# A low part made by the matmul engine, two convolutions moved back to the vector engine, and a new order: local and global attention with a gated layer on one core

## The chip, the cores and the metric

The kernel runs on one core of a Trainium2 chip. Its engines each work through an instruction stream of their own: TensorE (PE, with the weight load PEld ahead of each matmul), VectorE (DVE), ScalarE (ACT), GpSimd (POOL) and SyncE (SP, which here issues loads). The metric is the time of one execution in microseconds; before the change it is 375.08 us (median of 3 runs, 374.77 to 375.1).

## What is computed

```python
# attention: 8 batches, 8 heads, 512 local and 32 global positions, head size 64
s_g = scale * q_g @ concat(k_g, k_l).T            # global queries see everything
out_g = softmax(s_g) @ concat(v_g, v_l)
s_ll = where(|i - j| <= 32, scale * q_l @ k_l.T, -1e9)
a_l = softmax(concat(scale * q_l @ k_g.T, s_ll))  # local: global keys and a window
out_l = a_l @ concat(v_g, v_l)
x = concat(out_g, out_l) as [batch, 544, 512]     # heads side by side
# gated layer
gate = sigmoid(sum_k conv_w[k] * x shifted by 4 - k positions)   # 5 taps, causal, per channel
out = (gate * (x @ w_val)) @ w_out
```

(The shapes in the kernel: 512 local positions and 32 global ones of each batch.)

## The kernel before

The work is cut into 32 **units**: one batch and two of the eight heads, so four units make a batch. A unit u goes through these steps, which are named as in the order table (line numbers are those of the profile):

- `s` (L474): 32 small fp32 matmuls give the scores of 16 blocks of 32 queries against 128 keys, into two banks of PSUM. An fp32 matmul shows as two records in the trace, so 64 records a unit.
- `mx` (L486, DVE) adds the mask and finds the maximum, `exp` (L493, ACT) exponentiates, `t` (L499, PE) transposes with the identity into PSUM, `tc` copies that to SBUF (L306 if on ACT, L308 if on DVE), `av` (L510, PE) multiplies with the values.
- `eps` and `norm` (L521 and L523, DVE) divide by the sum, giving `xs`; `xt` (L529, PE) transposes it, channels to partitions, into a bank; `xc` copies the bank to SBUF behind four columns of `halo`.
- `xh` rounds that x to the matmul's fp32r format (the high part), and `xl` (L561, DVE) subtracts: the low part is x minus its high part. The gated layer multiplies high and low parts separately, three products for one.
- The convolution: for units 4 to 31 a `tap` and four `conv` steps (L565, DVE). For the first `NPC = 4` units it is done on PE instead: `dg` (L577, ACT) scales the identity by a tap five times, `pc` (L588) are five fp32 matmuls of 128x512 with these diagonals (two records each), and `pco` copies the sum to SBUF as the gate.
- `sig` (L596, ACT) makes the gate's tanh.

A batch's gated layer follows: `g1` (L612) are 4 x 4 groups of three matmuls of 128x512, `gv` (L620, DVE) multiplies with the gate, `gh` and `gl` (L626, DVE) split into high and low parts, and `g2` (L634) are again 4 x 4 groups of three, `ob` scales and `st` stores. The global queries of a batch have their own steps (`gs`, `gmax`, `gexp`, `gt`, `gtc`, `gav`, `gnorm`, `gx`). The weights arrive in 64-bit floats and are turned into two fp32r parts by steps `w0.s0` to `w7.s7`, on DVE and ACT, in the first 80 us.

What sets the order is a table written out by hand, `ORDER`: a list of step names, each with its engine where there is a choice (`:ACT`, `:DVE`) and the PSUM bank that it takes (`@n`). The program emits the steps in that order, and each engine runs its own steps in the order in which they stand there, waiting for what a step needs. A step also waits for room: there are eight PSUM banks, ten tiles each for xh, xl and gate, three for pm and mx, and loads take their turn by the table too (`iq`, `iv`, `wi`).

The low part, as it is before:

```python
(G if plan.tasks[f"xl{u}"].eng == "POOL" else V).tensor_tensor(out=xs_l[u],
    in0=st[u]["xc"][:, KW - 1:], in1=xs_h[u].bitcast(F32), op=ALU.subtract)
```

Of the kernel before, what the change touches and what calls it, by code (L numbers as in the profile page):

```python
# [51 lines left out]
tc0.0:ACT z1.0@3 t1.1@3 tc0.1:ACT tc1.1:ACT t1.0@4 w0.s4 av0@1 s2@57 wi4 w0.s5 w0.s6 eps0:ACT norm0 tc1.0:ACT xt0@4
xc0:ACT w0.s7 gs0@02 mx2.0 exp2.0 dg1 halo0 w1.s0:DVE w0.high:DVE mx2.1 iq4 pc0.0@6 pc0.1 pc0.2 gmax0.0 w1.s1 av1@4
s3@70 gmax0.1 w1.s2 gexp0.0 w1.s3 w1.s4 iq5 exp2.1 t2.1@1 eps1:DVE norm1 t2.0@2 xt1@3 tc2.1:ACT gt0.0@4 mx3.0 mx3.1
exp3.1 w1.high:ACT exp3.0 xc1:DVE xh1:ACT tc2.0:DVE pc0.3 pc0.4 halo1 pco0:ACT w1.s5 w1.s6 av2@2 t3.0@1 eps2:DVE norm2
pc1.0@7 pc1.1 xt2@2 w1.s7 w4.s0:DVE w4.s1 tc3.0:ACT w4.s2 w4.s3 gtc0.0 w4.s4 w3.s0:ACT w3.s1 gexp0.1 iq6 iq7 w4.s5 dg2
pc1.2 t3.1@3 tc3.1:ACT w4.high:ACT s4@10 mx4.0 mx4.1 av3@4 xc2:ACT w4.s6 w4.s7 xh0:ACT gav0.0@6 gt0.1@1 eps3:ACT norm3
pc1.3 gtc0.1 wi5 gav0.1 w3.s2 s5@34 exp4.1 t4.1@0 geps0:ACT w3.s3 gnorm0 exp4.0 gx0@1 gxc0:ACT mx5.0 mx5.1 halo2:DVE
tc4.1:ACT w3.s4 w3.s5 iv4 xt3@6 xc3:ACT xh3:ACT w5.s0:ACT w5.s1 xl3 t4.0@2 tc4.0:ACT pc1.4 pc2.0@5 pc2.1 pc2.2
w3.high:ACT exp5.0 xl0 pco1:ACT exp5.1 gs1@03 dg3 iv5 iv7 iv6 w5.s2 w5.s3 w5.high:DVE gmax1.0 gexp1.0 av4@6 gmax1.1  # L60
eps4:ACT t5.0@2 tc5.0:ACT pc2.3 pc2.4 s6@04 w5.s4 fix1 w5.s5 w5.s6 pco2:ACT sig2 t5.1@1 w5.s7 halo3:ACT pc3.0@3
gexp1.1 tc5.1:ACT norm4 xt4@6 xc4:ACT mx6.0 exp6.0 mx6.1 exp6.1 w3.s6 xl1 w3.s7 av5@1 eps5:ACT s7@05 mx7.0 gt1.0@6
gtc1.0 w2.s0:DVE fix0 sig0 norm5 w2.s1 xh2:DVE pc3.1 iq8 pc3.2 g1.0.0.0@4 wi6 t6.0@6 exp7.0 w2.s2 w2.s3 w2.s4 xt5@0
xc5:ACT mx7.1 t6.1@7 tc6.1:ACT pc3.3 pc3.4 w2.s5 tc6.0:ACT pco3:ACT w2.high:ACT w6.s0:ACT av6@1 gav1.0@0 w2.s6 w2.s7
eps6:ACT norm6 iq9 s8@76 exp7.1 xl2 t7.0@5 mx8.0 mx8.1 exp8.1 t7.1@3 wi7 gt1.1@1 w7.s0:ACT tc7.1:DVE exp8.0 w6.s1
w6.s2 gtc1.1 g1.0.0.1 g1.0.0.2 g1.0.0.3 gv.0.0 gh.0.0:ACT w6.s3 w6.high:ACT w6.s4 w7.s1 g1.0.1.0@7 g1.0.1.1 xt6@6 sig3
g1.0.1.2 g1.0.1.3 iq10 iq11 w7.s2 g1.0.2.0@4 g1.0.2.1 w7.s3 w7.high:ACT w7.s4 w7.s5 sig1 w7.s6 w7.s7 xc6:ACT g1.0.2.2
g1.0.2.3 gl.0.0 w6.s5 g1.0.3.0@2 g1.0.3.1 g1.0.3.2 gv.0.1 gv.0.2 tc7.0:ACT av7@5 w6.s6 w6.s7 eps7:ACT norm7 xh4:ACT
gav1.1 gh.0.1:DVE s9@31 iv8 geps1:ACT gnorm1 gs2@46 gx1@0 tap6:ACT iv9 mx9.0 exp9.0 gmax2.0 gl.0.1 g1.0.3.3 g2.0.0.0@3
gh.0.2:ACT t8.0@4 gv.0.3 gh.0.3:DVE t9.0@5 gxc1:ACT xt7@0 tap5:DVE tc8.0:ACT tc9.0:ACT t8.1@2 g2.0.0.1 halo5:ACT  # L70
gl.0.2 g2.0.0.2 gl.0.3 g2.0.0.3 g2.0.1.0@4 g2.0.1.1 mx9.1 g2.0.1.2 iv11 exp9.1 tc8.1:ACT gexp2.0 conv5.0 xc7:DVE
tap7:ACT halo6:DVE t9.1@5 ob.0.0:ACT iq12 st.0.0 iv10 tc9.1:ACT g2.0.1.3 g2.0.2.0@2 ob.0.1:ACT conv6.0 conv6.1
halo7:DVE conv7.0 g2.0.2.1 gt2.0@0 gtc2.0 iq13 gmax2.1 st.0.1 conv5.1 g2.0.2.2 av8@3 eps8:ACT xh5:ACT conv6.2 conv6.3
conv5.2 conv5.3 av9@0 eps9:ACT norm8 s10@56 xl5 mx10.0 xt8@3 g2.0.2.3 g2.0.3.0@7 g2.0.3.1 g2.0.3.2 xh7:ACT g2.0.3.3
xh6:ACT exp10.0 norm9 t10.0@4 mx10.1 exp10.1 halo4:ACT conv7.1 iq14 t10.1@5 s11@01 xl6 ob.0.3:ACT iq15 gav2.0@7
tc10.1:ACT tc10.0:ACT tap4:DVE conv4.0 conv4.1 xt9@6 xl4 gexp2.1 gt2.1@4 sig5 mx11.0 g1.1.0.0@0 conv4.2 sig6 gtc2.1
gav2.1 geps2:ACT av10@4 xl7 conv4.3 sig4 eps10:ACT xc8:ACT xh8:ACT gnorm2 gx2@7 g1.1.0.1 g1.1.0.2 g1.1.0.3 xc9:ACT
xh9:ACT tap9:ACT ob.0.2:DVE g1.1.1.0@6 st.0.2 gxc2:DVE halo9:ACT norm10 st.0.3 mx11.1 exp11.1 tap8:DVE conv7.2 conv7.3
g1.1.1.1 g1.1.1.2 g1.1.1.3 g1.1.2.0@2 gv.1.0 gv.1.1 gh.1.0:DVE gl.1.0 t11.1@7 gh.1.1:ACT g1.1.2.1 gl.1.1 gs3@30
gmax3.0 s12@56 mx12.0 mx12.1 exp11.0 tc11.1:ACT t11.0@7 gexp3.0 g1.1.2.2 g1.1.2.3 g1.1.3.0@3 g1.1.3.1 xt10@4  # L80
# [833 lines left out]
```

## Time and profile before

| | |
|---|---|
| median of 3 runs | 375.08 us |
| profiled execution | 375.27 us |
| its span, first to last instruction | 373.5 us |
| PE busy | 359.2 us (96% of the span), 6349 matmul records |
| DVE busy | 317.9 us (85%) |
| ACT busy | 227.9 us (61%) |
| POOL busy | 0.8 us |
| DMA | 66.7 MB, mean 179 GB/s |

The span is the stretch from the first to the last instruction; what lies around it is 1.8 us. "Busy" counts an engine as busy while any of its instructions runs; matmuls are pipelined and their ends are modelled, so a matmul's own duration is longer than the step from one to the next, and the step is what a sum must use. In the chain of waits, "issue" is time in which an engine waited for nothing that the profile shows.

### The profile page before, as it was taken

What the parts mean: (1) busy time and instruction counts of PE and PEld (TensorE: products, weight loads), DVE (VectorE), ACT (ScalarE), POOL (GpSimd) and SP (SyncE); (2) the same over time, 40 slices, a digit from 0 to 9 for tenths busy, and PEclk for the clock granted to TensorE, in tenths of its full rate; (3) what the DMA queues carried; (4) which work ended last, traced back from release to release, by engine and by line L of the source; (5) the groups of instructions that cost most, each with busy time, mean ns of one, the idle gap of its engine ahead of it and who ended that gap; (6) DMA issues with size and microseconds to landing.
All of it is one profiled execution on the core that took longest, in us unless ns stands there. A gap on an engine that the chain in (4) does not pass through costs nothing.

```text
span 373.5 us, 14728 instructions
## 1 busy us (share of the span) xinstructions
PE 359.2 (96%) x6349; PEld 282.3 (76%) x6349; DVE 317.9 (85%) x1045; ACT 227.9 (61%) x586; POOL 0.8 (0%) x7
## 2 busy tenths in 40 slices
PE   7899989989899998999999999999999999999995
PEld 4566556868687886887877888888878888888894
DVE  4899888799988996999998897897889898797972
ACT  4789886476587375876568754685375567354040
POOL 0000000000000000000000000000000000000000
PEclk9999999999999999999999999999999999999999
DMA  7996584546841565942762854472920501011113
GB/s 280 400 396 221 167 323 134 162 153 220 352 146 52 193 217 224 333 186 107 259 237 68 320 218 162 184 270 90 336 85 32 215 4 58 2 56 73 42 65 105
DMA packets 17249, 66.74 MB, mean 179 GB/s; under 512 B 1952, under 2 KB 4000, under 8 KB 17184
## 3 DMA queue, kind: packets, MB, share of 16 engines
q1 hardware_dynamic: 12240, 57.12, 42.3%
q10 hardware_dynamic: 4944, 8.67, 6.4%
q8 instruction: 50, 0.82, 0.9%
q14 instruction: 15, 0.12, 0.1%
HBM read 56.87 MB, written 8.91 MB: 176 GB/s over the span
## 4 chain that ended last, share of the span: by engine, by line
PE 90%; DMA 4%; issue 2%; ACT 2%; SPq 1%; DVE 0%; DVEq 0%; ACTq 0%
PE psum L634 25%; PE psum L612 23%; PE psum L510 9%; PE psum L474 8%; PE psum L499 8%; PE psum L588 5%; PE psum L529 4%; DMA v<-in_vw_dram 3%; PE psum L439 3%; PE psum L400 2%; DMA wraw<-in_w_out_dram 2%; PE psum L419 2%; PE psum L421 1%; SPq L324 1%; PE psum L455 0%
## 5 line engine op out<-in xcount | busy, mean ns | idle before, releaser
L493 ACT ACTIVATE pm<-pm,mx 128x128 f32<-128x128 f32 x256 | 80.5, 392 | 14.6 <-DVE mx L486 14.2
L565 DVE SCALAR_TENSOR_TENSOR gate<-xc,cw,gate 128x512 f32<-128x512 f32 x112 | 82.8, 748 | 2.0
L486 DVE CUSTOM_DVE_ANT_0 pm<-psum,mask 128x128 f32<-128x128 f32 x256 | 57.3, 285 | 5.2 <-PE psum L474 5.1
L612 PE MATMUL psum<-xh,wvh 128*128 128x512 f32 x128 | 53.7, 419 | 0.0
L634 PE MATMUL psum<-woh,gh 128*128 128x512 f32 x128 | 52.6, 411 | 0.0
L634 PE MATMUL psum<-woh,gl 128*128 128x512 f32 x128 | 50.2, 392 | 1.5 <-issue 1.5
L634 PE MATMUL psum<-wol,gh 128*128 128x512 f32 x128 | 50.2, 392 | 1.4 <-issue 1.4
L612 PE MATMUL psum<-xl,wvh 128*128 128x512 f32 x128 | 50.6, 396 | 0.0
L612 PE MATMUL psum<-xh,wvl 128*128 128x512 f32 x128 | 50.1, 391 | 0.0
L499 PE MATMUL psum<-ident,pm 128*128 128x128 f32 x256 | 40.8, 280 | 0.3 <-issue 0.3
L474 PE MATMUL psum<-qk 64*32 64x128 f32 x2048 | 38.1, 278 | 1.9 <-issue 1.5
L306 ACT COPY pts<-psum 128x512 f32<-128x512 f32 x50 | 28.4, 582 | 18.3 <-PE psum L499 17.9
L510 PEld LDWEIGHTS psum<-v,pts 128*32 128x32 f32 x2048 | 30.5, 109 | 11.3 <-issue 4.6
L499 PEld LDWEIGHTS psum<-ident,pm 128*128 128x128 f32 x256 | 29.8, 140 | 9.9 <-issue 3.1
L510 PE MATMUL psum<-v,pts 128*32 128x65 f32 x2048 | 35.2, 221 | 1.9 <-ACT pts L306 1.2
L474 PEld LDWEIGHTS psum<-qk 64*32 64x32 f32 x2048 | 29.5, 107 | 9.6 <-issue 4.3
L299 ACT ACTIVATE ob<-psum 128x512 f32<-128x512 f32 x25 | 14.8, 595 | 28.3 <-PE psum L634 26.7
L634 PEld LDWEIGHTS psum<-wol,gh 128*128 128x128 f32 x128 | 24.2, 189 | 5.8 <-issue 1.8
L634 PEld LDWEIGHTS psum<-woh,gh 128*128 128x128 f32 x128 | 24.2, 189 | 5.8 <-issue 1.7
L612 PEld LDWEIGHTS psum<-xh,wvl 128*128 128x128 f32 x128 | 24.0, 188 | 5.5
L612 PEld LDWEIGHTS psum<-xh,wvh 128*128 128x128 f32 x128 | 24.2, 189 | 5.1 <-ACT pgt L427 0.4
L634 PEld LDWEIGHTS psum<-woh,gl 128*128 128x128 f32 x128 | 24.0, 188 | 5.2
(114 smaller groups left out, 541.9 us busy)
## 6 DMA issues: line engine op xcount, KB each, us to landing
v<-in_vw_dram SPq DMA_DIRECT2D x32, 975.0 KB, 6.2
qk<-in_qk_dram SPq DMA_DIRECT2D x32, 624.0 KB, 5.4
out_dram<-ob ACTq DMA_DIRECT2D x32, 256.0 KB, 2.3
wraw<-in_w_val_dram SPq DMA_DIRECT2D x4, 512.0 KB, 12.2
...
```

The lines of the kernel that those rows point to most:

```text
L299: A.activation(out=out, in_=in_, func=AF.Copy, scale=by)
L306: A.copy(out, in_)
L474: on_pe(T.matmul((sx, sy)[h][32 * j:32 * j + 32, i, :], qkt[rows, 32 * m:32 * m + 32], qkt[rows, k0:k0 + P], start=True, stop=True))
L486: V.tensor_tensor_reduce(out=pm[:, h, i, :], in0=s[:, i, :], in1=mask[:, i, :], op0=ALU.add, op1=ALU.min, scale=-SCALE, scalar=3.0e38, acc ...
L493: A.activation(out=pm[:, h, i, :], in_=pm[:, h, i, :], func=AF.Exp, bias=mx[:, c:c + 1], scale=-1.0)
L499: on_pe(T.transpose(pt[:, i, :], pm[:, h, i, :], ident))
L510: on_pe(T.matmul(ax[32 * j:32 * j + 32, h, E1 * i:E1 * i + E1], pts[:, h, i, 32 * j:32 * j + 32], vt[:, block_win(4 * i + j), h, :], start ...
L529: on_pe(T.transpose(xt[:, P * i:P * i + P], xs[:, i].rearrange("p h d -> p (h d)"), ident))
L565: V.scalar_tensor_tensor(out=acc, in0=xc[:, k:k + SL], scalar=cw[:, u % NDT, k:k + 1], in1=acc, op0=ALU.mult, op1=ALU.add)
L588: on_pe(T.matmul(st[u]["pc"], diag[(u * KW + k) // NDT][:, (u * KW + k) % NDT, :], st[u]["xc"][:, k:k + SL], start=(k == 0), stop=(k == KW ...
L612: on_pe(T.matmul(box["pv", e], w[:, e, t * P:t * P + P], x, start=(t == 0 and q == 0), stop=(t == NDT - 1 and q == 2)))
L634: on_pe(T.matmul(box["po", r], g[:, e, rs], w[:, e, :], start=(e == 0 and q == 0), stop=(e == NDT - 1 and q == 2)))
```

## The change

Three things change.

**The low part of the first eight units.** The transposition `xt` of units 0 to 7 leaves its bank's sum open. When `xh` is there, a new step `xn` multiplies the high part with a negative identity (one fp32r matmul of 128x512) and adds the product to the same bank, which then holds x minus its high part. `xl` of these units becomes a copy of that bank to SBUF, in all eight on ACT. The bank is given back after `xl`, not after `xc`.

**Two units' convolution.** `NPC` goes from 4 to 2. Units 2 and 3 get a `tap` and four `conv` steps like the later ones, and their `dg`, `pc` and `pco` are gone.

**A new order.** All names of the table stand in a new order, 141 steps (the eight `xl` among them) stand on the other one of ACT and DVE, and PSUM banks are given out anew. The warm-up matmuls ahead of the first attention product (`z`) are three instead of one. (Code paths for `GP` and `p_sigmoid` are added, but `GP` is empty and no unit takes the other.)

```diff
 ORDER = """
-cw dg0 s0@61 s1@52 mx0.0 mx0.1 exp0.0 t0.0@6 mx1.0 mx1.1 exp0.1 t0.1@0 exp1.1 w0.s0:DVE w0.s1 w0.s2 w0.s3 exp1.0
...
+cw s0@15 s1@70 mx0.0 exp0.0 mx0.1 mx1.0 mx1.1 t0.0@1 exp0.1 exp1.0 z2.0@2 t1.0@3 exp1.1 tc1.0:ACT w0.s0:DVE w0.s1
...
-NPC = 4
+NPC = 2
 WO = 2
+XP = range(0, 8)
+GP = range(0, 0)
...
+    nident = cp.tile([P, P], F32R, name="nident")
...
     def l_xt(u):
         xt, xs = bank(f"xt{u}"), st[u]["xs"]
         for i in range(4):
-            on_pe(T.transpose(xt[:, P * i:P * i + P], xs[:, i].rearrange("p h d -> p (h d)"), ident))
+            on_pe(T.matmul(xt[:, P * i:P * i + P], xs[:, i].rearrange("p h d -> p (h d)"), ident, start=(i == 0 or u not in XP),
+                     stop=(u not in XP), is_transpose=True, skip_group_check=u in XP))
...
+    def l_xn(u):
+        on_pe(T.matmul(bank(f"xt{u}"), nident, xs_h[u], start=False, stop=True, skip_group_check=True))
+
     def l_xl(u):
+        if u in XP:
+            copy(f"xl{u}", xs_l[u], bank(f"xt{u}"))
+            return
         (G if plan.tasks[f"xl{u}"].eng == "POOL" else V).tensor_tensor(out=xs_l[u], in0=st[u]["xc"][:, KW - 1:], in1=xs_h[u].bitcast(F32), op=ALU.subtract)
...
-        plan.add(f"xc{u}", ("ACT", "DVE"), lambda u=u: l_xc(u), [f"xt{u}"], take=[("xc", u)], give=[("bank", f"xt{u}")])
+        plan.add(f"xc{u}", ("ACT", "DVE"), lambda u=u: l_xc(u), [f"xt{u}"], take=[("xc", u)], give=[] if u in XP else [("bank", f"xt{u}")])
...
-        plan.add(f"xl{u}", ("DVE", "POOL"), lambda u=u: l_xl(u), [f"xh{u}"], lock=True)
+        if u in XP:
+            plan.add(f"xn{u}", "PE", lambda u=u: l_xn(u), [f"xh{u}"])
+            plan.add(f"xl{u}", ("ACT", "DVE"), lambda u=u: l_xl(u), [f"xn{u}"], give=[("bank", f"xt{u}")])
+        else:
+            plan.add(f"xl{u}", "DVE", lambda u=u: l_xl(u), [f"xh{u}"], lock=True)
...
+        G.tensor_scalar(out=nident, in0=ident, scalar1=-1.0, scalar2=None, op0=ALU.mult)
```

The lines of the changed kernel are numbered anew: `xn` is L565 there, `conv` L575, `pc` L598, `g1` L626, `gl` L646, and the copies L309 (ACT) and L311 (DVE).

Three places of the order. First PE behind the global scores of batch 1 (the 16 matmuls of L400 just ahead), before the change: the convolution of unit 2 (`xc_675`) and the first matmul of unit 3's (`xc_810`) stand among the attention steps of units 4 to 7. An "x2" counts two fp32 matmuls.

```order
L510 MATMUL psum<-v_804,pts_634 32x65 x32
L499 MATMUL psum<-ident,pm_770 128x128 x4
L588 MATMUL psum<-xc_675,diag_589 128x512 x2
L474 MATMUL psum<-qk_582 32x128 x32
L499 MATMUL psum<-ident,pm_770 128x128 x4
L588 MATMUL psum<-xc_810,diag_589 128x512
L529 MATMUL psum<-ident,xs_974 128x128 x4
L510 MATMUL psum<-v_863,pts_772 32x65 x32
L474 MATMUL psum<-qk_584 32x128 x32
```

The same place of PE after it: behind batch 1's global scores and unit 4's attention product.

```order
L513 MATMUL psum<-v_767,pts_633 32x65 x32
L502 MATMUL psum<-ident,pm_812 128x128 x4
L626 MATMUL psum<-xh_665,wvh 128x512
L626 MATMUL psum<-xl_666,wvh 128x512
L626 MATMUL psum<-xh_665,wvl 128x512
L626 MATMUL psum<-xh_817,wvh 128x512
L626 MATMUL psum<-xl_818,wvh 128x512
L626 MATMUL psum<-xh_817,wvl 128x512
L502 MATMUL psum<-ident,pm_812 128x128 x4
L532 MATMUL psum<-ident,xs_938 128x128 x4
L477 MATMUL psum<-qk_515 32x128 x32
L513 MATMUL psum<-v_857,pts_814 32x65 x32
```

The convolutions are gone, and the first products of batch 0's gated layer stand in their place; in the table before the change they begin after the scores of unit 7.

Second, PE at the new product of unit 0, after the change (`xh_399` is unit 0's high part, `xc_372` its x).

```order
L598 MATMUL psum<-xc_372,diag_291 128x512 x2
L502 MATMUL psum<-ident,pm_336 128x128 x4
L565 MATMUL psum<-xh_399,nident 128x512
L513 MATMUL psum<-v_96,pts_194 32x65 x32
L477 MATMUL psum<-qk_93 32x128 x32
L502 MATMUL psum<-ident,pm_336 128x128 x4
L532 MATMUL psum<-ident,xs_485 128x128 x4
```

Between unit 0's transposition and its `xn` stand the global scores of batch 0, two convolution matmuls and half a transposition; the next attention product is queued behind `xn`.

Third, DVE ahead of the normalisation of unit 11 (L521 and L523), before the change.

```order
L308 COPY pts_1809<-psum 128x512
L407 ISA pg_1_2129,gm_1_2128<-psum,zero 128x544
L407 ISA gm_1_2128 128x1
L308 COPY xc_2146<-psum 128x512
L620 SCALAR_TENSOR_TENSOR gv_2_2148<-gate_1476,psum 128x512
L308 CAST xh_2150<-xc_2146 128x512
L301 TENSOR_SCALAR gate_2156<-xc_2146,cw 128x512
L314 TENSOR_SCALAR mx_1808<-psum 128x8
L521 RECIPROCAL mx_1808<-mx_1808 128x8
L523 TENSOR_TENSOR xs_2168<-psum,mx_1808 128x512
```

And after it, where the normalisation is L524 and L526:

```order
L489 ISA pm_2165,mx_2166<-psum,mask 128x128
L489 ISA mx_2166 128x1
L317 TENSOR_SCALAR mx_1855<-psum 128x8
L311 COPY pts_1982<-psum 128x512
L524 RECIPROCAL mx_1855<-mx_1855 128x8
L526 TENSOR_TENSOR xs_2211<-psum,mx_1855 128x512
L575 SCALAR_TENSOR_TENSOR gate_1779<-xc_1737,cw,gate_1779 128x512
L646 TENSOR_TENSOR gl_2065<-gv_1_2077,gh_2064 128x512
```

Unit 13's maxima now stand ahead of unit 11's normalisation, and two low parts `gl` of batch 1 (in the table before, ahead of it) behind it.

## Rows read from the trace of the kernel before

**Rows 1.** Busy time of the engines in three stretches, and their clock (PEclk).
```profile
20.00:40.00 20.00, 18.80 (x515) 12.96 (x514) 17.80 (x68) 16.19 (x46) 0.00 (x0) 1.00 0.79 289
140.00:160.00 20.00, 18.53 (x469) 15.42 (x468) 16.38 (x63) 13.11 (x37) 0.00 (x0) 1.00 0.76 289
160.00:180.00 20.00, 20.00 (x404) 15.95 (x403) 19.31 (x64) 14.84 (x38) 0.00 (x0) 1.00 0.32 114
```

**Rows 2.** The chain that ended last, by engine, then pieces: start, us, what.
```profile
PE 90%; DMA 4%; issue 2%; ACT 2%; SPq 1%; DVE 0%; DVEq 0%; ACTq 0%
...
3.67 10.63 DMA v<-in_vw_dram
14.44 1.15 PE psum L510 x64
...
41.50 3.44 PE psum L588 x8
...
336.23 11.12 PE psum L612 x48
```

**Rows 3.** Groups of instructions by line: count, busy us, mean ns of one.
```profile
L588 PE MATMUL psum<-xc,diag 128*128 128x512 f32 x40 | 19.0, 598 | 0.0
...
L565 DVE SCALAR_TENSOR_TENSOR gate<-xc,cw,gate 128x512 f32<-128x512 f32 x112 | 82.8, 748 | 2.0
L561 DVE TENSOR_TENSOR xl<-xc,xh 128x512 fp32r<-128x512 f32 x32 | 21.7, 684 | 0.2
L308 DVE COPY xc<-psum 128x512 f32<-128x512 f32 x9 | 6.2, 686 | 2.5 <-PE psum L529 2.5
L308 DVE CAST xh<-xc 128x512 fp32r<-128x512 f32 x10 | 4.2, 422 | 0.1
L306 ACT COPY gate<-psum 128x512 f32<-128x512 f32 x4 | 2.3, 582 | 0.6 <-PE psum L588 0.6
```

**Rows 4.** Timeline of PE: start, us, what, and the idle time before it.
```profile
38.11 0.73 PE L439 MATMUL psum<-v,pgt 96*32 96x65 f32 x34 [1.20 <-issue]
...
55.50 0.77 PE L474 MATMUL psum<-qk 64*32 64x128 f32 x37 [1.45 <-issue]
...
101.53 0.50 PE L634 MATMUL psum<-wol,gh 128*128 128x512 f32 x1 [1.39 <-issue]
...
146.64 0.39 PE L634 MATMUL psum<-woh,gl 128*128 128x512 f32 x1 [1.47 <-issue]
```

**Rows 5.** Instructions of PE and PEld up to each idle time; the instruction queue.
```profile
0.00:37.50 37.50, 33.73 (x731) 20.74 (x732) 29.63 (x135) 27.18 (x76) 0.85 (x7) 1.00 0.86 323
0.00:54.90 54.90, 49.66 (x1114) 30.93 (x1115) 45.13 (x196) 42.24 (x118) 0.85 (x7) 1.00 0.82 303
0.00:100.90 100.90, 92.99 (x1879) 64.55 (x1879) 85.57 (x331) 71.45 (x195) 0.85 (x7) 1.00 0.71 257
0.00:146.00 146.00, 136.56 (x2772) 100.01 (x2773) 125.43 (x464) 100.20 (x267) 0.85 (x7) 1.00 0.65 232
...
q8 instruction: 50, 0.82, 0.9%
```

**Rows 6.** Timeline at the attention product of unit 7 and the transposition of unit 11.
```profile
77.90 0.59 ACT L306 COPY pts<-psum 128x512 f32<-128x512 f32 x1
...
78.54 1.11 PE L510 MATMUL psum<-v,pts 128*32 128x65 f32 x64 [1.22 <-ACT pts L306]
...
124.31 0.69 DVE L523 TENSOR_TENSOR xs<-psum,mx 128x512 f32<-128x512 f32 x1
...
129.35 0.66 PE L529 MATMUL psum<-ident,xs 128*128 128x128 f32 x4
```

**Rows 7.** Who waited for whom, 7 to 125 us: us in total, times, longest.
```profile
DVE pm L486 <- PE psum L474: 3.2, 4, 1.6
DVE wa L271 <- ACT wa L266: 2.2, 2, 1.9
...
DVE gd L449 <- ACT gd L312: 1.3, 2, 0.7
```

More of the change, by code (lines that the diff above doesn't have):

```diff
@@ L50 @@
 ORDER = """
-cw dg0 s0@61 s1@52 mx0.0 mx0.1 exp0.0 t0.0@6 mx1.0 mx1.1 exp0.1 t0.1@0 exp1.1 w0.s0:DVE w0.s1 w0.s2 w0.s3 exp1.0
[L52 to L80, printed above, removed]
@@ L593, in p_conv_out, with p_sigmoid @@
         copy(f"pco{u}", gates[u], st[u]["pc"])
+    def p_sigmoid(u):
+        gates[u] = sb.tile([P, SL], F32, tag="gate", name=f"gate{u}", bufs=NX)
+        A.activation(out=gates[u], in_=bank(f"pc{u}"), func=AF.Tanh, scale=0.5)
     def sigmoid(g):
@@ L623, in gh, with gn @@
             copy(f"gh.{key}.{e}", box["gh"][:, e, :], box["gv", e])
+        def gn(e):
+            on_pe(T.matmul(box["pv", e], nident, box["gh"][:, e, :], start=False, stop=True, skip_group_check=True))
         def gl(e):
+            if key in GP:
+                copy(f"gl.{key}.{e}", box["gl"][:, e, :], box["pv", e])
+                return
             V.tensor_tensor(out=box["gl"][:, e, :], in0=box["gv", e], in1=box["gh"][:, e, :].bitcast(F32),
@@ L651, in moe @@
                 last = name
-            plan.add(f"gv.{key}.{e}", "DVE", lambda e=e: gv(e),
-                     [last] + deps_gate(e) + ([f"gv.{key}.{e - 1}"] if e else []),
-                     take=[("gv", f"{key}.{e}")] + ([("g", key)] if e == 0 else []),
+            gvd = [last] + deps_gate(e) + ([f"gv.{key}.{e - 1}"] if e else [])
+            gt = [("g", key)] if e == 0 else []
+            if key in GP:
+                plan.add(f"gv.{key}.{e}", "DVE", lambda e=e: gv(e), gvd, take=gt, give=[("gate", x0 + e)])
+                plan.add(f"gh.{key}.{e}", ("ACT", "DVE"), lambda e=e: gh(e), [f"gv.{key}.{e}"])
+                plan.add(f"gn.{key}.{e}", "PE", lambda e=e: gn(e), [f"gh.{key}.{e}"])
+                plan.add(f"gl.{key}.{e}", ("ACT", "DVE"), lambda e=e: gl(e), [f"gn.{key}.{e}"],
+                         give=[("bank", f"g1.{key}.{e}")])
+                continue
+            plan.add(f"gv.{key}.{e}", "DVE", lambda e=e: gv(e), gvd, take=[("gv", f"{key}.{e}")] + gt,
                      give=[("bank", f"g1.{key}.{e}"), ("gate", x0 + e)])
@@ L778, in attention_moe @@
                          take=[] if k else [("bank", f"pc{u}")], give=diagonals(u)[1] if k == KW - 1 else [])
-            plan.add(last, ("ACT", "DVE"), lambda u=u: p_conv_out(u), [f"pc{u}.{KW - 1}"], take=[("gate", u)], give=[("bank", f"pc{u}")])
+            if u < NHF:
+                plan.add(last, ("ACT", "DVE"), lambda u=u: p_conv_out(u), [f"pc{u}.{KW - 1}"], take=[("gate", u)], give=[("bank", f"pc{u}")])
+            else:
+                last = f"pc{u}.{KW - 1}"
         else:
@@ L794, in attention_moe @@
         for u in units:
+            if NHF <= u < NPC:
+                plan.add(f"sig{u}", "ACT", lambda u=u: p_sigmoid(u), [f"pc{u}.{KW - 1}"], take=[("gate", u)],
+                         give=[("bank", f"pc{u}")])
+                continue
             plan.add(f"sig{u}", "ACT", lambda u=u: sigmoid(gates[u]),
-                     [f"fix{u}" if u < NHF else f"pco{u}" if u < NPC else f"conv{u}.{KW - 2}"])
+                     [f"fix{u}" if u < NHF else f"conv{u}.{KW - 2}"])
         last = moe(b, SL, 4 * b, lambda t, b=b: [f"xl{4 * b + t}"], lambda e, b=b: [f"sig{4 * b + e}"], last,
```

181 lines of the change are left out of this document (105 added, 76 removed).

## The prediction

> **What bounds the kernel now.** I read the busy time of the engines by stretches first. From 160 us on PE is busy for 20.00 of 20 us; between 20 and 160 us it misses 1.2 to 1.5 us in a stretch of 20 [rows 1]. The granted clock is 1.00 in all three, the upper of its two levels (2.4 GHz). So PE sets the time almost everywhere, but VectorE is close behind it (19.31 of 20 us in one stretch), and in the first 80 us ScalarE is too (16.19 of 20).
>
> The chain that ended last says the same: 90% of it is PE, 4% a load at the start, 2% "issue" and 2% ScalarE [rows 2]. That load is the first v tile: it lands at 14.30, and the first attention product starts at 14.44 [rows 2]. Nothing that PE does earlier is worth anything.
>
> Then I looked for PE's idle time behind 14.44. Four idle times of 1.20, 1.45, 1.39 and 1.47 us have no other engine as their cause [rows 4]. The instructions of PE and PEld up to them are 1463, 2229, 3758 and 5545 [rows 5], so 766, 1529 and 1787 lie between: three, six and seven times 256, less the few semaphore instructions that this view leaves out. The instruction queue moved 0.82 MB in 50 packets [rows 5], 16 KB each. I read this as PE waiting for its next block of instructions. The one large wait for another engine is 1.22 us at unit 7's attention product, for ScalarE's copy [rows 6]. So of 375 us little is waiting on PE, and a cut in its work should show, unless PE then waits for VectorE or ScalarE.
>
> **PE's work.** Removed: the convolutions of units 2 and 3, five fp32 matmuls of 128x512 each, which is 20 of the 40 records of that line [rows 3]. The duration of 598 ns is not the step: eight of them back to back took 3.44 us, 0.43 us each [rows 2]. 20 x 0.43 = 8.6 us off. Added: eight `xn`, one record each, of the shape and type of the gated layer's products; 48 of these took 11.12 us, 0.23 each [rows 2]. 8 x 0.23 = 1.85 us. Their weight load overlaps like the layer's. The two extra warm-up matmuls lie ahead of 14.44, in the wait for v, and cost nothing; if that wait were gone they would cost under 1 us. The transpositions keep their number and shape, so opening the sum is taken at nothing. Net -6.75 us, and it lies between 14 and 90 us, where PE still has idle time.
>
> **VectorE's work.** Added: eight convolution steps at 82.8 / 112 = 0.74 us, 5.9. Removed: eight subtractions at 21.7 / 32 = 0.68 us, 5.4 [rows 3]. Of the steps that change sides it gets five more roundings `xh` (2.1), three more output scalings (2.1 at the 0.69 of a copy from PSUM), and loses two `xc` copies (1.4), three taps (1.3 at the price of `xh`), three first weight steps (1.3) and some small ones (1.1) [rows 3]. The sum is -0.4: VectorE has as much to do as before.
>
> **ScalarE's work.** It loses two sets of diagonals and two gate copies of 0.58 us [rows 3] and gets eight copies for the low part at about the same price (4.7), five taps more, five roundings fewer. Some 3 us more, at 61% busy over the span. That is hidden behind PE later on, but not by itself in the first 80 us.
>
> **The order.** What matters is how much each engine must do ahead of the places where PE needs the others. I counted the steps of both tables up to two of them.
>
> At unit 11's transposition PE has 11.8 us less ahead of it than before: ten convolution matmuls (8.6), five groups of three products of the gated layer (5 x 0.695 = 3.5), one attention product (1.1) and one global transposition (0.5) less, eight `xn` more. VectorE, up to the normalisation which that transposition needs, has the same amount as before within 0.7 us: twelve convolution steps and two maxima more, five low parts, three `xc`, three taps, five of the splits gh and gl and some conversions fewer. Before, `xs` ended at 125.0, and the transposition started at 129.35, 4.35 us later [rows 6], so VectorE had slack there. Now PE by its own work would be there at 129.35 - 11.8 = 117.6. If VectorE came no earlier than before (125.0 - 0.7 = 124.3), PE would stand still for 6.7 us, and the whole gain would be gone.
>
> At unit 7's attention product PE has 10.4 us less ahead of it, while ScalarE, up to the copy for it, has 0.9 us less. The copy ended at 78.49 and PE waited 1.22 us [rows 6]. By its own work PE would now be there at 78.54 - 1.22 - 10.4 = 66.9.
>
> So the gain is 6.75 us less the larger of these two delays (PE waits once for both: a delay at unit 7 shifts PE towards VectorE at unit 11). How much earlier can the two engines come? Only by waiting less. VectorE was idle for 15.3 us up to 100.9, 7.9 of it up to 37.5 [rows 5], nearly all of that the start, which stays; 7.4 us lie behind it, and some 2 more up to 125. Between 7 and 125 us, 3.2 us were waits of the maxima for PE's scores, which shrink as PE runs ahead; 2.2 were waits for a weight step that itself waited for a load, and 1.3 for ScalarE in the global part [rows 7]; these may stay. I take half of the 9.4 as gone: `xs` at 119.6, a delay of 2.0. ScalarE was idle for 12.7 us up to 54.9 [rows 5], 8 of it the start; if of all its idle time up to 78 some 9 us go (waits for PE and for late weight loads, which the new table issues earlier against their use), its copy ends at 68.6 and the delay is 1.7, near VectorE's. The ends: every wait stays (a delay of 6.7 by VectorE, of over 10 by ScalarE), or none is felt (0). I take 2.2.
>
> **Instruction blocks.** In the new table PE's instructions of the first 145 us are packed closer, since the long convolution matmuls are half gone: counted in blocks of 256 and by PE's steps, five blocks behind the start hold under 4.2 us of work, where three did. Two of those three ended in such an idle time, and so did two longer ones [rows 4]. Between none of the four and three more, that is -5.5 to +4.2 us at 1.4 each. I take no difference, since a block that comes late while PE waits for VectorE anyway costs nothing twice. The Trainium skill, "Runtime: NRT & Kernel Launch", section "Instruction fetch mechanics", also gives blocks of 16 KiB or 256 instructions, and says that their fetch is hidden because instructions are issued more slowly than they arrive. By that rule closer packing could cost nothing, and the upper end of this term would be 0 instead of +4.2; the four idle times at multiples of 256 speak against it, so the end stays.
>
> **The sum.** -6.75 + 2.2 = -4.55. It is made against the profiled execution, 375.27 us (span 373.5 and 1.8 around it), which is 0.2 us above the median. From the median of 375.08: 370.5 us.
>
> **The rivals.**
>
> *PE's gain in full.* VectorE and ScalarE come early enough, and one or two late blocks or the wait at unit 7 go too: -6.75 to -9, 366 to 368.6 us. For it: in the table nearly all of VectorE's waits up to 125 us come from PE or are small. Against it: 19 of 20 us is the most that VectorE reached in any stretch shown.
>
> *VectorE becomes the bound.* It keeps its waits, the normalisation of unit 11 ends at 122 to 124.3, and 4.5 to 6.7 us of the gain are lost: 372.6 to 375.3 us. For it: the same work ahead of the same step. Against it: the waits for PE's scores have no reason left.
>
> *Slower: ScalarE at unit 7.* If its copy for unit 7 still ends near 77.6 (as before, less 0.9), PE waits there for 10.7 us, 3.95 more than the change saves: 379 us. It decides from 73.7 on (66.9 + 6.75): a copy that ends later than that makes the kernel slower. For it: ScalarE now carries the eight low parts, and each stands behind an `xn` on PE's queue, which itself stands ahead of the attention product or transposition queued next, so engines can hold each other up; it does nothing before the first exponential, where it used to make diagonals. Against it: over half of its idle time was waiting for others that now come earlier.
>
> *The product costs more than it says.* Were `xn` two records of 0.43 like the fp32 convolution, 8 x 0.63 = 5.0 us would be lost, and the time were 375.5 us. The high part and the negative identity are both fp32r, as in the gated layer, which speaks against it.
>
> **How the numbers follow.** The forecast (368.6 to 372.6) has 0.50, the gain in full 0.17, VectorE as the bound 0.17, ScalarE slower 0.13, the dear product 0.03. What can be told from no change is 0.2%, 0.75 us: faster is below 374.3, slower above 375.8. Faster: 0.50 + 0.17 + 0.10 of VectorE's case = 0.77. Same: the rest of that case, 0.07, and 0.02 of the dear product = 0.09. Slower: 0.13 + 0.01 = 0.14. The range goes from 367.0, which leaves out 0.04 of the fullest gain, to 374.8, which leaves out the slower cases and a little of "same".
>
> **What would show it.** In the profile after: 20 records of the convolution line at 0.43 us a step, and eight of `xn` at 0.23; PE busy some 6 to 7 us less; the transposition of unit 11 directly behind its `xs`, near 120 us, and not with 4 us between; ScalarE's copy for unit 7 near 69 us; idle times by "issue" of about 1.4 us, three to six of them; from about 170 us on PE without a gap. I am wrong if PE's idle time between 60 and 150 us grows by more than 6 us, if a stretch of it is granted the lower clock, or if the idle times by "issue" are more than seven.

## The result, and the profile after

The changed kernel takes 369.62 us (median of 4 runs, 369.41 to 370.3), the kernel before beside it 374.92 us. The ratio is 0.9873, with an interval of 0.9839 to 0.9906: 5.3 us faster, against 4.55 forecast. 369.62 us lies near the forecast of 370.5 and within its range. The profiled execution took 369.67 us, its span is 367.6 us (373.5 before).

The page of the kernel after: busy times, the clock in 40 slices, and the chain by engine. The lines that answer to [rows 2] and [rows 3] are the chain and the line L598 (which was L588).

```profile
PE 351.7 (96%) x6339; PEld 281.4 (77%) x6339; DVE 316.3 (86%) x1042; ACT 229.1 (62%) x587; POOL 1.6 (0%) x8
...
PEclk9999999998999999999999999999999999999999
...
PE 87%; DMA 4%; DVE 4%; issue 2%; ACT 1%; SPq 1%; DVEq 0%
```

```profile
L598 PE MATMUL psum<-xc,diag 128*128 128x512 f32 x20 | 9.6, 601 | 0.1
...
L565 PE MATMUL psum<-xh,nident 128*128 128x512 f32 x8 | 3.8, 474 | 0.0
```

PE has 7.5 us less to do, VectorE and ScalarE hardly differ. One slice of PE's clock, the tenth, shows less than full speed; before, none did.

Where PE still waits, by its timeline (start, us, what, and in brackets the idle time before it and what ended it); this answers to [rows 4]:

```profile
27.26 0.99 PE L513 MATMUL psum<-v,pts 128*32 128x65 f32 x52 [1.06 <-issue]
33.39 0.42 PE L477 MATMUL psum<-qk 64*32 64x128 f32 x7 [0.55 <-issue]
50.19 0.63 PE L502 MATMUL psum<-ident,pm 128*128 128x128 f32 x4 [0.44 <-DVE xs L526]
82.81 0.41 PE L477 MATMUL psum<-qk 64*32 64x128 f32 x4 [2.53 <-issue]
...
168.96 0.39 PE L626 MATMUL psum<-xh,wvh 128*128 128x512 f32 x1 [0.64 <-issue]
...
232.07 0.40 PE L477 MATMUL psum<-qk 64*32 64x128 f32 x2 [0.39 <-issue]
...
295.56 0.54 PE L442 MATMUL psum<-v,pgt 96*32 96x65 f32 x20 [1.39 <-issue]
```

Almost all of it is "issue" again: 6.6 us in six pieces, where [rows 4] had 5.5 in four. For another engine PE waits here 0.44 us (and 0.23 at the start); before, ScalarE's copy alone cost 1.22 [rows 6].

Busy times around the longest of these (PE, PEld, DVE, ACT, POOL with their counts; then granted clock, DMA share, GB/s):

```profile
76.88:80.28 3.40, 3.40 (x130) 2.56 (x129) 3.37 (x13) 3.40 (x10) 0.00 (x0) 1.00 1.03 428
80.28:82.81 2.53, 0.01 (x1) 0.00 (x0) 2.39 (x7) 1.15 (x4) 0.00 (x0) 1.00 1.00 406
82.81:84.00 1.19, 1.19 (x9) 0.99 (x8) 1.19 (x8) 0.00 (x0) 0.00 (x0) 0.65 0.99 416
84.00:86.00 2.00, 2.00 (x7) 1.61 (x6) 1.08 (x12) 0.00 (x0) 0.00 (x0) 0.50 0.34 133
86.00:87.00 1.00, 1.00 (x4) 0.78 (x4) 0.00 (x0) 0.99 (x3) 0.00 (x0) 0.71 0.00 0
```

PE stands still for 2.53 us while loads move at over 400 GB/s, and right behind it the granted clock is the lower of the two levels (0.50, that is 1.2 GHz, from 84 to 86 us), until about 87 us. What that costs is the missing share of each stretch: 1.19 x 0.35 + 2.00 x 0.50 + 1.00 x 0.29 = 1.7 us.

**The account of the span.** PE's work, by the prediction's count: -6.75. Waits for VectorE and ScalarE: 1.54 before (1.22 and one of 0.32 at the start), 0.67 after: -0.9. "Issue": 6.6 for 5.5: +1.0. Lower clock: +1.7. The first attention product starts 0.3 us earlier (14.12 for 14.44): -0.3. Together -5.2; measured: -5.9 for the span, -5.6 for the profiled time. What is missing lies in PE's work: from the first attention product to the last matmul, without the idle times and the loss by the clock, PE's own time is 347.6 us before and 340.0 after, 7.6 less and not 6.75. Why it is that much was not followed up.

### The profile page after: what moved, and what is told of

It reads as the page before. It is cut to its first block, busy times and chain, and to the rows that moved or that the text cites. A ratio compares the mean times of both kernels' runs of the same rounds, so it can differ in the third digit from the quotient of the medians.

```text
span 367.6 us, 14708 instructions
## 1 busy us (share of the span) xinstructions
PE 351.7 (96%) x6339; PEld 281.4 (77%) x6339; DVE 316.3 (86%) x1042; ACT 229.1 (62%) x587; POOL 1.6 (0%) x8
## 4 chain that ended last, share of the span: by engine, by line
PE 87%; DMA 4%; DVE 4%; issue 2%; ACT 1%; SPq 1%; DVEq 0%
PE psum L654 26%; PE psum L626 24%; PE psum L513 8%; PE psum L477 8%; PE psum L502 7%; PE psum L532 4%; DMA v<-in_vw_dram 3%; PE psum L442 3%; PE psum L598 2%; PE psum L422 2%; PE psum L403 1%; DMA wraw<-in_w_out_dram 1%; PE psum L424 1%; DVE pm L489 1%; SPq L327 1%
## 5 line engine op out<-in xcount | busy, mean ns | idle before, releaser
L575 DVE SCALAR_TENSOR_TENSOR gate<-xc,cw,gate 128x512 f32<-128x512 f32 x120 | 88.0, 749 | 6.3 <-ACT gate L302 3.8
L496 ACT ACTIVATE pm<-pm,mx 128x128 f32<-128x128 f32 x256 | 80.6, 392 | 15.4 <-DVE mx L489 14.7
L626 PE MATMUL psum<-xh,wvh 128*128 128x512 f32 x128 | 53.2, 416 | 0.6 <-issue 0.6
L626 PE MATMUL psum<-xl,wvh 128*128 128x512 f32 x128 | 50.8, 397 | 0.0
L626 PE MATMUL psum<-xh,wvl 128*128 128x512 f32 x128 | 50.1, 392 | 0.0
L477 PE MATMUL psum<-qk 64*32 64x128 f32 x2048 | 37.2, 273 | 4.8 <-issue 3.5
L502 PE MATMUL psum<-ident,pm 128*128 128x128 f32 x256 | 38.1, 279 | 0.8 <-DVE xs L526 0.4
L477 PEld LDWEIGHTS psum<-qk 64*32 64x32 f32 x2048 | 29.2, 105 | 11.5 <-issue 6.9
L309 ACT COPY pts<-psum 128x512 f32<-128x512 f32 x50 | 28.2, 584 | 10.8 <-PE psum L502 10.3
L626 PEld LDWEIGHTS psum<-xl,wvh 128*128 128x128 f32 x128 | 24.1, 189 | 5.5 <-issue 1.5
L626 PEld LDWEIGHTS psum<-xh,wvl 128*128 128x128 f32 x128 | 24.0, 188 | 5.5
L626 PEld LDWEIGHTS psum<-xh,wvh 128*128 128x128 f32 x128 | 24.2, 189 | 5.1 <-issue 0.7
```

The source lines that it names most:

```text
L309: A.copy(out, in_)
L477: on_pe(T.matmul((sx, sy)[h][32 * j:32 * j + 32, i, :], qkt[rows, 32 * m:32 * m + 32], qkt[rows, k0:k0 + P], start=True, stop=True))
L496: A.activation(out=pm[:, h, i, :], in_=pm[:, h, i, :], func=AF.Exp, bias=mx[:, c:c + 1], scale=-1.0)
L502: on_pe(T.transpose(pt[:, i, :], pm[:, h, i, :], ident))
L575: V.scalar_tensor_tensor(out=acc, in0=xc[:, k:k + SL], scalar=cw[:, u % NDT, k:k + 1], in1=acc, op0=ALU.mult, op1=ALU.add)
L626: on_pe(T.matmul(box["pv", e], w[:, e, t * P:t * P + P], x, start=(t == 0 and q == 0), stop=(t == NDT - 1 and q == 2)))
```

## The experiments

Two questions were left. What is each part of the change worth? And what are the idle times by "issue" of PE, which cost more than any wait for another engine? The second turned out to spoil the answers to the first, until it was understood. In all kernels PE's queue is counted in **entries**: matmul records, weight loads, and the few semaphore instructions that the windows leave out but the trace holds.

**1. Without the product: n_noxn.** The new order, but the low parts of units 0 to 7 are subtracted on VectorE, as for the others.

```diff
-XP = range(0, 8)
+XP = range(0, 0)
 (ORDER: xn0 to xn7 taken out; xl0 to xl7 lose their :ACT)
```

> The changed kernel with one part undone: units 0 to 7 get their low part by VectorE's subtraction again (at the place in the order where the copy stood), the eight products with the negative identity are gone. PE has 8 x 0.23 = 1.85 us less, VectorE 8 x 0.68 = 5.4 us more, ScalarE eight copies less. Theory A (the time follows PE's work, and VectorE is covered): 369.6 - 1.85 = 367.8 us. Theory B (VectorE is the next bound: after the change, unit 11's transposition starts 0.1 us behind its xs, so all that VectorE gets more ahead of it is waited for): up to 5.4 us of waits come back, 371 to 373.2 us, and the transposition of unit 11 starts 3 to 5 us later than at 118.4.

Measured: 366.79 us, ratio 0.981 (0.9771 to 0.985). Faster than the change, and by more than any theory gave, which is why it was run once more beside the changed kernel (n_noxn_b, after_ctl):

> The changed kernel once more, unaltered, beside the other three on one chip. Theory A (the blocks of instructions come late behind the loads): 369.6 us, with the idle time of 2.5 us at 82.8 and the lower clock behind it in its profile. Theory B (the subtraction kernel gained 2.8 us only because it ran on another chip): this one and the subtraction kernel come within 1 us of each other here.

> The new order with all low parts subtracted on VectorE and no xn, once more, beside the changed kernel on one chip. Theory A (xn costs PE 1.85 us and draws PE's instructions closer to the place where the block comes late): 366.8 us, 2 to 3.5 us under the changed kernel beside it. Theory B (chip): within 1 us of the changed kernel.

Measured: the changed kernel 370.03 us (368.67 to 371.58), without the product 366.64 us (365.86 to 370.44), and 373.98 for the kernel before. So the difference of some 3 us is no matter of the chip. Who made PE wait without the product (waits of PE: us in total, times, longest):

```profile
PE psum L442 <- issue: 1.7, 1, 1.7
...
PE psum L477 <- issue: 1.3, 1, 1.3
PE psum L502 <- DVE gm L410: 1.2, 1, 1.2
PE psum L502 <- ACT mx L315: 1.2, 1, 1.2
PE psum L532 <- DVE xs L526: 0.7, 2, 0.5
...
PE psum L532 <- DVE gm L410: 0.6, 1, 0.6
PE psum L403 <- DVE xs L526: 0.5, 1, 0.5
```

VectorE has 5.4 us more to do here, and PE waits for it: 3.0 us in the lines above without the one on ACT's mx, which falls on a block's boundary (below). (A wait of 0.67 for ScalarE at 10.39 us is left out, since PE still waits for v behind it.) Beside it the changed kernel waited 0.6 for other engines behind the first attention product, and

```profile
PE psum L477 <- issue: 3.0, 3, 2.0
PE psum L513 <- issue: 1.5, 1, 1.5
...
PE psum L442 <- issue: 0.8, 1, 0.8
PE psum L626 <- issue: 0.6, 1, 0.6
```

5.9 by issue, against 4.5 without the product (1.7, 1.3, the 1.2 at mx, and one of 0.28), and the lower clock on top. The eight `xn` took 2.6 us by the steps to what followed them, and 1.8 by the difference of PE's own time in the two traces (340.3 and 338.5, counted as in the account above). So the product by itself saves 2.4 of waits for 1.8 to 2.6 of work, about nothing either way; it is blocks and clock (1.5 + 1.7) that made the kernel with it the slower one. This split is worked out from the two traces, not shown by a run of its own: the kernel without the product was not run with its blocks shifted (part 4).

**2. The loads: n_loads, n_noxn_loads.** Is it the loads in flight that hold the block at 82.81? Three loads that end there are issued later.

```diff
 (ORDER: iq12 and iq13 moved from behind g1.0.3.3 to just before iq14,
  iv11 from behind w7.s3 to behind g2.0.1.3; in both kernels alike)
```

> The changed kernel with three loads of 67 to 77 us issued later (both parts of q for 12 and 13 until just before that of 14, v for 11 behind the output group g2.0.1.3), all else alike. Theory A (the block of instructions at 82.8 waits behind the queued loads, and the lower clock follows from that wait): the idle time of 2.53 us and the 1.7 us of lower clock go, 365.5 to 367.5 us. Rival (the late block has nothing to do with the loads, or the wait turns up at the next block): 369 to 370 us, with an idle time of over 1.5 us by issue between 75 and 100 us again.

> The new order without xn, with the same three loads issued later. It had no late block near 82 us, so by theory A the loads have nothing to give back: 366.3 to 367.3 us, as without the move. Rival (the loads slow something else there, for instance the weight steps or v): 364 to 366 us.

Measured: n_loads took 371.48 us (369.87 to 374.58), the changed kernel beside it 370.03 (368.67 to 371.58). n_noxn_loads took 368.06 us (median of three runs, 367.27 to 368.93; a fourth took 373.05), and without the move 366.64 (365.86 to 370.44). So the move gained nothing; that it cost something is not clear of the noise. But the trace of n_loads says that the place itself behaved in good part as theory A had it (timeline of PE, then windows as above):

```profile
81.51 0.41 PE L477 MATMUL psum<-qk 64*32 64x128 f32 x4 [1.15 <-issue]
95.54 1.09 PE L513 MATMUL psum<-v,pts 128*32 128x65 f32 x32 [2.52 <-ACT ob L302]
```

```profile
80.00:84.00 4.00, 2.85 (x41) 2.08 (x28) 3.86 (x13) 2.02 (x7) 0.00 (x0) 1.00 0.03 10
...
95.54:97.00 1.46, 1.46 (x56) 1.46 (x60) 1.46 (x4) 1.43 (x4) 0.00 (x0) 0.50 0.53 191
```

With hardly a load left, the idle time is 1.15 us instead of 2.53 and the clock behind it stays at the upper level. What was won is lost at 95.54: the moved loads now lie ahead of a store of the output (issued at 87.64, landed at 94.81, with the loads at 300 to 430 GB/s from 86 to 93 us), ScalarE waits for that store's buffer, PE waits for ScalarE:

```profile
94.89 0.60 ACT L302 ACTIVATE ob<-psum 128x512 f32<-128x512 f32 x1 [3.28 <-DMA out_dram<-ob]
```

and behind that wait of 2.52 us, which has nothing to do with instruction blocks, the clock falls in the same way. So loads lengthen a late block, they are not its cause, since 1.15 us stay without them. The sum is a miss for both theories (365.5 to 367.5, or 369 to 370): the loads only changed what they collide with, in n_noxn_loads too, where the same wait at 95.54 is 1.61 us.

**3. The convolution: o_conv, n_pc4, n_order.** The move of units 2 and 3 to VectorE alone, in the order of before (o_conv); and the reverse, the new order with their convolution back on PE, with the product (n_pc4) and without (n_order).

```diff
 o_conv: -NPC = 4  +NPC = 2, ORDER of before without dg2, dg3, pc2.*, pc3.*;
         tap2, conv2.0, conv2.1 behind xh2, tap3 behind xh3, the rest among g1.0.0.* and g1.0.1.*
 n_pc4:  -NPC = 2  +NPC = 4, new ORDER with
         av4 pc2.0 pc2.1 pc2.2 ... pc2.3 pc2.4 ... g1.0.0.2 pc3.0 pc3.1 g1.0.0.3 pc3.2 pc3.3 pc3.4 ... s6
```

> The kernel before with one part of the change: the convolutions of units 2 and 3 go from PE to VectorE, in the old order (their steps stand around the first products of batch 0's layer), low parts by subtraction. PE 8.6 us less, VectorE 5.9 us more. Theory A (PE's work alone decides): 375.1 - 8.6 = 366.5 us. Theory B (VectorE has only 4.35 us of slack at unit 11 in the old order, and less before it): most of the 8.6 us is lost in waits for VectorE, 371 to 375 us.

> The changed kernel with the other part undone: the convolutions of units 2 and 3 are on PE again (20 records of 0.43 us, PE 8.6 us more, VectorE 8 x 0.74 = 5.9 us less), put between unit 4's attention product and unit 4's transposition of the new order. Theory A: 369.6 + 8.6 = 378.2 us, less what PE waited anyway, 376.5 to 378.2. Theory B (VectorE bounds the first 120 us): the 8.6 us fill time in which PE waits for VectorE, 370 to 373 us.

> The new order alone: low parts by VectorE's subtraction and four convolutions on PE, as before, in the new order. Against the changed kernel PE has 6.75 us more and VectorE about the same. Theory A (the gain is PE's work): 369.6 + 6.75 = 376.4 us, so the order alone is no faster than the kernel before, 375 to 377. Rival (the order itself brings most of the gain): 370 to 372 us.

Measured: o_conv 378.06 us (374.22 for the kernel before beside it), ratio 1.0083 (1.0057 to 1.0109), slower than before and over both expectations, although PE has 8.6 us less to do. Its PE waits:

```profile
PE psum L532 <- DVE xs L526: 3.6, 2, 2.3
PE psum L513 <- ACT pts L309: 3.4, 2, 1.9
PE psum L513 <- ACT pm L496: 2.0, 1, 2.0
...
PE psum L403 <- DVE xs L526: 1.2, 1, 1.2
```

In the old order the 5.9 us of convolution stand on VectorE where PE needs it. Behind the first attention product PE waits 10.8 us for VectorE and ScalarE (1.5 before) and loses 3.4 us by the lower clock, at 14.7 and at 62.5 us; its idle times by issue are shorter (2.4 for 5.5). So it gives back more than it saved. n_pc4 took 388.68 us and n_order 388.83: 19 us over the changed kernel, far outside both expectations. My placing is one cause to think of: ten fp32 products stand in PE's queue ahead of the scores of unit 6, and VectorE has nothing to do meanwhile:

```profile
62.65 0.29 DVE L489 CUSTOM_DVE_ANT_0 pm<-psum,mask 128x128 f32<-128x128 f32 x1 [10.10 <-PE psum L477]
```

But idle time of VectorE costs only what PE then waits for it, and more of the 19 us lies in the waits of PE by issue in n_pc4, up to 3.0 us each:

```profile
PE psum L477 <- issue: 8.9, 4, 3.0
```

By the two traces the span of n_pc4 is 19.0 us longer: 8.7 of PE's own work, 6.2 by issue (12.7 for 6.6), 1.7 of lower clock, 2.1 of waits for other engines, and a start 0.3 later.

**4. Blocks of 256: ph32, ph232, pc4_ph148, before_ph64.** Counted in entries, every long idle time by issue of every kernel here stands at the same place of a block: 961, 1217, 3521, 7105, 9409 and 11713 in the kernel after, 1473, 2241, 3777 and 5569 before, 961, 1217, 5569, 6081, 7105, 10177, 11713 and 12225 in n_pc4; each is a multiple of 256 plus 193. The windows of the kernel after show it but for the semaphore instructions (counts of PE and PEld between one idle time and the next):

```profile
27.24:33.36 6.12, 5.58 (x127) 3.97 (x127) 4.76 (x12) 4.96 (x13) 0.00 (x0) 1.00 0.95 379
33.36:82.78 49.42, 46.44 (x1147) 35.39 (x1147) 46.97 (x182) 45.00 (x119) 0.00 (x0) 1.00 0.67 261
82.78:168.94 86.16, 85.32 (x1786) 70.58 (x1786) 79.37 (x280) 65.51 (x168) 0.00 (x0) 0.98 0.55 198
168.94:295.54 126.60, 124.66 (x2293) 101.87 (x2293) 111.16 (x351) 72.58 (x190) 0.00 (x0) 1.00 0.47 168
```

254, 2294, 3572 and 4586 entries, with 2, 10, 12 and 22 semaphore instructions: 1, 9, 14 and 18 blocks. If that is the cause, a few instructions more at the very start, where PE waits for q anyway, must move all boundaries onto other work. Four kernels do only that:

```diff
-        keep_clock(2, 7, zf)
+        keep_clock(1, 7, zf)
+        for n in range(9):
+            j = n % 4
+            on_pe(T.matmul(psum[32 * j:32 * j + 32, 7, :64], zf[:, :32], zf[:, :64], start=True, stop=True))
```

This is ph32: a warm-up product of 4 entries goes, nine tiny ones of 4 entries each come, 32 entries more. ph232 has none of the two and 60 tiny ones, pc4_ph148 the same with 39 in n_pc4, before_ph64 keeps one and has 17, in the kernel before.

> The changed kernel with one of its two first warm-up products replaced by nine tiny ones (64 columns), all before the first scores and so in time that PE waits for q: the same work later, but every later instruction of PE stands 32 places further back in its queue. Theory A (blocks of 256: PE's idle times by issue stand where a block, counted over all entries of its queue, took less than 5.9 to 6.4 us with loads running or 3.1 to 3.6 us without): the boundaries now fall on other work, 13 blocks are too short instead of 7, their sum goes from 8.8 to 24.7 us by this count (6.2 measured for the first), so 376 to 386 us, with idle times near 24, 53, 67, 129, 143, 166, 231, 249 and 294 us. Theory B (the idle times belong to the loads or to the work at those places): 369 to 370.5 us, idle at 27, 33 and 82 as before.

> The same with both warm-up products replaced by sixty tiny ones, which shifts PE's queue by 232 places. Theory A: the short block before 82.8 us is gone, the sum of the idle times falls from 8.8 to 5.2 by the count, and the lower clock behind 82.8 (1.7 us) goes with it: 365.5 to 367.5 us. Theory B: 369 to 370.5 us.

> The new order with the convolution of units 2 and 3 put back on TensorE (388.7 us), with both warm-up products replaced by 39 tiny ones, a shift of 148 places. Its own trace had idle times by issue of 2.97, 2.99, 2.47, 1.22 and 0.87 us at 139, 181, 268, 313 and 327 us, each at a block's boundary. Theory A: by the count the idle sum falls from 13.5 to 5.2 us, and the lower clock behind each goes too: 377 to 381 us, that is the 8.6 us of products, the wait of VectorE at 62 us and nothing more. Theory B (it was slow by the place of the products alone): 387 to 390 us.

> The kernel before, its order and work untouched, with one of its two first warm-up products replaced by seventeen tiny ones, a shift of PE's queue by 64 places. Theory A (blocks of 256): by the count of its own trace the idle sum goes from 4.2 to 27.6 us, the largest near 23, 35, 53, 97, 109 and 143 us, in its own places and not in those of the changed kernel; the changed kernel's shift by 32 gave 0.8 of the counted sum, so about 393 us, between 384 and 400. Theory B (only the new order is open to this): 374 to 376 us.

| kernel | shift | expected by blocks | measured | same kernel unshifted |
|---|---|---|---|---|
| ph32 | 32 | 376 to 386 | 382.36 (380.07 to 384.99) | 369.6 to 370.0 |
| ph232 | 232 | 365.5 to 367.5 | 366.66 (365.09 to 368.81) | 369.6 to 370.0 |
| pc4_ph148 | 148 | 377 to 381 | 378.13 (376.85 to 381.19) | 388.7 |
| before_ph64 | 64 | 384 to 400, about 393 | 391.76 (388.47 to 392.89) | 374.0 to 374.9 |

All four times came out as the blocks have it, in both directions, with the same work on every engine behind the start. The count behind the forecasts was rougher than the times: it had 24.7 us by issue for ph32 and 27.6 for before_ph64, where 15.1 and 15.4 came, and it left out the lower clock, which cost ph32 some 6 us more than the unshifted kernel. That the two errors nearly cancel there is luck. In ph32 the first attention product starts at 14.02 us as ever, so the tiny products cost nothing; then (timeline of PE, and waits)

```profile
27.02 2.92 PE L598 MATMUL psum<-xc,diag 128*128 128x512 f32 x3 [2.38 <-issue]
58.85 0.32 PE L513 MATMUL psum<-v,pts 128*32 128x65 f32 x1 [3.37 <-issue]
```

```profile
PE psum L477 <- issue: 7.2, 3, 2.8
PE psum L513 <- issue: 3.4, 1, 3.4
PE psum L598 <- issue: 2.4, 1, 2.4
PE psum L442 <- issue: 1.8, 2, 0.9
```

15.1 us by issue, and the lower clock behind most of the long ones:

```profile
58.85:62.00 3.15, 3.15 (x11) 2.62 (x12) 1.05 (x2) 1.99 (x5) 0.00 (x0) 0.50 0.73 295
```

Of nine places named for ph32, six came (the work that stood at 24, 53, 129, 166, 249 and 294 us), and one at 324 us that was not named; 67, 143 and 231 did not. In before_ph64 four of six came. So a short block is needed for a long idle time, but does not always bring one. Some blocks and the idle time that followed (work is PE's busy time between the two boundaries, idle the rest):

```
kernel        boundary at   work since the last   idle   loads in that time
after           82.81 us       3.40 us            2.53      419 GB/s
n_loads         81.51          3.43               1.15      238
after           27.26          4.99               1.06      389
before_ph64     26.89          3.24               3.50      391
after          295.56          2.25               1.39       77
after           65.17          3.37               none        5
after          193.99          3.32               none      111
before_ph64     60.57          4.02               none      423
```

Where the block was late, work and idle time together come to 5.9 to 6.7 us with loads at about 400 GB/s and to 3.1 to 3.6 with few, with exceptions either way (the last line; n_noxn at 35.11 us, 1.86 us behind a block of 5.4).

What decides can be read from the same traces, in the packets of the instruction queue (on the page of the kernel after: packets, MB, share of the DMA engines).

```profile
q8 instruction: 49, 0.80, 0.9%
```

There is one of 16 KB for each block behind the first boundary, so they can be put beside the boundaries in order. In the 14 kernels, at 682 boundaries, PE never goes on sooner than 1.0 us after the end of the packet that belongs there; at the 74 of them where it had stood idle for 0.3 us or more, it went on 1.0 to 1.6 us after that end. At 82.81, for instance, the packet ran from 80.24 to 81.35 us. So these are waits for instructions. The packet itself takes 0.9 to 1.6 us at these 74; what varies is when it begins. Counted from PE's entry into the block before, that is at the median 0.7 us where less than 10 GB/s were moved meanwhile, and 3.5 us where more than 350 were (up to 5.0); 3.1 at 82.81 in the changed kernel, and 1.9 at the same place in n_loads. The exceptions fit too: 4.75 us at 35.11 in n_noxn, and 0.8 in the last line of the table. Why that packet began so soon beside 423 GB/s is open.

The shifts also bear on the move of the convolutions in part 3. With the blocks shifted, the new order with the two convolutions on PE takes 378.13 us and the changed kernel 366.66, 11.5 us apart; the spans of the two profiled executions (379.2 and 363.3) are 15.9 apart. Of these, 7.9 are PE's own work, 1.5 waits for other engines, 0.3 a later start, and 6.3 are late blocks and lower clock that the shift by 148 left or brought (4.00 us at 20.48, 2.36 at 177.66). So in the new order the move itself is worth some 9.7 us, an estimate from these two traces. In the old order it was worth nothing (o_conv). And the order with the product, without the move of the convolutions, is slower than the kernel before (378.13 against 374.42, ratio 1.0113, 1.0056 to 1.0169).

Faster than both kernels are n_noxn (366.79 and 366.64) and ph232 (366.66).

## Why the prediction came out right, and where its steps were not

**PE's work: right, a little small.** 20 records of the convolution line and eight of `xn`; busy time fell by 7.5 us, -6.75 had been counted. The `xn` had a step of 0.23 to 0.43 us to what followed, 0.33 on average and not 0.23, 0.8 us more than counted in all; by the difference of two traces (n_noxn_b) they cost 1.8 us, as counted.

**Where it lies: right.** The transposition of unit 11 was to be reached at 117.6 by PE's own work; it started at 118.43. From there to the end of the span it is 249.2 us, against 244.15 before, and 5.05 (11.8 - 6.75) of work had moved behind it, which makes 249.2. That it fits so well is partly luck: behind that point PE stood idle by issue for 2.4 us (0.64, 0.39 and 1.39, so the forecast of no gap from 170 us on failed twice), where it was 1.47 before, and its own work must have been shorter than counted by as much, 0.9 us. Ahead of it PE came 0.8 us later than the count, 0.5 of it by lower clock (+1.7), fewer waits for other engines (-0.9) and an earlier start (-0.3).

**The waits for VectorE and ScalarE: wrong, by their whole size.** They were to cost 2.0 to 2.2 us, and at the two places named they cost nothing. Here is the place (timelines of VectorE, PE and ScalarE), which answers to [rows 6]:

```profile
117.57 0.69 DVE L526 TENSOR_TENSOR xs<-psum,mx 128x512 f32<-128x512 f32 x1
```

```profile
118.20 0.39 PE L626 MATMUL psum<-xh,wvl 128*128 128x512 f32 x1
...
118.43 0.60 PE L532 MATMUL psum<-ident,xs 128*128 128x128 f32 x4
```

```profile
65.35 0.61 ACT L309 COPY pts<-psum 128x512 f32<-128x512 f32 x1
```

`xs` ends at 118.3 (119.6 forecast, 125.0 before), 0.2 us ahead of its transposition, and PE has work up to there. ScalarE's copy for unit 7 ends at 66.0 (68.6 forecast) and PE starts on it without a wait. So `xs` came 6.7 us earlier than before, 1.3 earlier than forecast, and PE came 0.8 later. Which term was wrong is told by VectorE's busy time (the third engine of the row) up to the end of `xs`, before and after:

```profile
0.00:125.00 125.00, 116.39 (x2338) 83.60 (x2339) 105.93 (x397) 86.94 (x234) 0.85 (x7) 1.00 0.64 229
```

```profile
0.00:118.26 118.26, 109.14 (x2383) 81.33 (x2383) 103.43 (x405) 97.66 (x255) 1.56 (x8) 0.99 0.71 269
```

VectorE's idle time fell from 19.1 to 14.8 us: "half of the 9.4 as gone", 4.7, was near the 4.2 that went. The step that failed is its work, "the same amount as before within 0.7 us": busy time fell by 2.5. The durations of its instructions up to there add up to the same (130.0 and 129.9 us), so more of them overlapped. What waits went was as the rival of the full gain had it: waits for PE from 5.5 to 1.7 us (7 us to the end of `xs`), since PE came sooner. Those for ScalarE stayed in sum, 5.4 and 5.9, but are others; the largest now is for the `tap` steps that ScalarE got:

```profile
DVE gate L575 <- ACT gate L302: 3.8, 2, 3.3
```

In ph232 and n_noxn, too, `xs` ends 0.2 us ahead of this transposition, at 115.9 and 120.1 us: it moves with PE. That VectorE was near its limit was true all the same: with 5.4 us more (n_noxn_b) PE waits 3.0 us for it.

**Instruction blocks: read rightly, priced wrongly.** The prediction took the idle times for late blocks of 256, which the shifts have now shown, and kept its bounds of -5.5 to +4.2 us. But it took no difference, from a count of short blocks, and it did not ask which loads run beside them, nor what the clock does behind a long one. Measured: six idle times of 0.39 to 2.53 us where three to six of about 1.4 had been named, +1.0 in all, and +1.7 of lower clock. The lower clock was on its own list of what would show it wrong, and it came, at 84 us. That these 2.7 us, put at nothing, came in place of the 2.2 us forecast for the waits is why the total agrees; it is luck in its parts.

**The bounds were too narrow for what the term can do.** The same work with the boundaries elsewhere gave 366.7 and 382.4 us. -5.5 to +4.2 holds the first, not the second. The Trainium skill ("Runtime: NRT & Kernel Launch", "Instruction fetch mechanics") has the fetch hidden behind the execution; the prediction weighed that and held it against the rows, and ph32 and before_ph64, with 15 us of such idle time each, agree with the rows and not with the Trainium skill.

**The rivals.** The gain in full (366 to 368.6) is what the change gives when its blocks fall well: ph232. VectorE as the bound did not come, and ScalarE at unit 7 did not: its copy ended 7.7 us ahead of the 73.7 from which it decides. The dear product did not.
